# Window attention on one core: 256 key tiles computed off ScalarE in two other ways

## The chip, the cores and the metric

One core of one Trainium2 chip. The metric is the device time of one execution in microseconds (us); lower is better. The engines are named as the profile names them: PE is TensorE (matmuls), PEld its weight loads, DVE is VectorE, ACT is ScalarE, POOL is GpSimd, SP is SyncE (here it only starts DMAs). PSUM holds what PE computes, in eight banks; POOL works on SBUF alone.

## What is computed

An image of 224 x 224 positions with 96 channels. Channels 0 to 47 attend within horizontal stripes of 8 rows, channels 48 to 95 within vertical stripes of 8 columns; a stripe has 1792 tokens, and each direction has 28 stripes.

```python
qkv = jnp.einsum('bhwc,cd->bhwd', x, wqkv)
...
ah = _softmax(jnp.einsum('bqc,bkc->bqk', qh, kh) * scale, axis=-1)
oh = jnp.einsum('bqk,bkc->bqc', ah, vh).reshape(B, H, W, C2)
...
av = _softmax(jnp.einsum('bqc,bkc->bqk', qv, kv) * scale, axis=-1)
ov = jnp.einsum('bqk,bkc->bqc', av, vv).reshape(B, nw, H, sw, C2)
...
return jnp.einsum('bhwc,cd->bhwd', o, wo)
```

The exponentials dominate: 56 stripes of 1792 x 1792 scores.

## The kernel before

**Tiles.** The work runs over 28 passes P, each with two stripes side by side (14 passes for the rows, 14 for the columns). In a pass the queries come in four chunks c of 512, 512, 512 and 256, and the 14 key blocks of 128 make 14 tiles a chunk (7 in the last, which takes two key blocks a tile). A tile is 128 keys x 512 queries x 2 stripes: 1024 numbers on each of 128 partitions. There are 28 x 49 = 1372 tiles.

**Tiles of ScalarE (1121 of them).** `do_q` emits the four score matmuls (L761) into one of two pairs of PSUM banks (0 and 1, or 2 and 3), and one ACTIVATE (L939) that writes 2 to the power of the score into one of `NPT` buffers `PT`, in bf16. `do_v` (L788) later multiplies `PT` by V and adds into the accumulator bank of the chunk.

**The other tiles (251).** They have their bits put together by DVE and POOL. `KINDS[P][c]` lists them, one letter a tile. Their scores come from L774 (`do_s`), into two of the four banks 4 to 7 (`RING`), with some rows more in the product that add constants, so that the low 16 bits of the fp32 in PSUM are the fraction of the exponent.

- Kind P (155 tiles): DVE makes q, an affine of the low 16 bits, in a buffer `qb` (`p1`, L1082); POOL squares it (L1110), adds a constant (L1111), squares again (L1106); PE computes the scores a second time with another constant; DVE adds 128 times the score to the correction and rounds to the 16 bits of a bf16 (`f`, L1087).
- Kind R (96 tiles): DVE makes q (L1082) and, in a second pass, the product of q with another affine (`p2`, L1084); POOL squares once (L1106); then the second scores and `f` as with P.
- Kinds W and Q are in the code and are not used (`NGB = 0`).

**What sets the order.** `ORDER` is one string per pass that writes PE's order out by hand: `q` a tile of ScalarE, `v` a product with V, `1` and `2` the first and second scores of another tile into two single banks (DVE then works in two halves of 512), `3` and `4` the same into two neighbouring banks (one DVE instruction of 1024), `k`, `g`, `f` the projections, the output projection and the final sums (`K` a pair of them). Between two letters a planner runs in Python as the kernel is built: it keeps a due time for each engine from constants such as `D_SQ` or `D_AF`, and from them chooses the order of the work on DVE (`dve_step`) and POOL (`pool_step`). The constants never run on the chip; they set orders alone. Every engine's queue is in order, and semaphores hold an instruction until its inputs are there.

A product with V needs 128 rows of PE and a score 64, so PE alternates between two tilings: letters q, 1 to 4 and f are one, v, k and g the other. POOL also does the normalisation of finished stripes (L1045), and SP starts the loads, transposes and stores.

## Time and profile before

| | |
|---|---|
| median of 3 runs | 1047.13 us (1046.86 to 1047.49) |
| profiled execution, its own time | 1047.03 us |
| its span, first to last instruction | 1045.2 us |
| busy: PE, DVE, ACT, POOL | 1024.8, 1027.6, 1034.9, 1001.9 us |
| ACTIVATEs of tiles (L939) | 1121, 1030.3 us together |
| tiles off ScalarE | 251 (155 P, 96 R) |
| DMA | 96.84 MB, mean 93 GB/s |
| granted TensorE clock | 0.999 |

A row of instruction groups reads: line, engine, operation, output <- inputs, shapes, count | busy time of the group, mean ns of one | idle time of the engine just before them, and what ended it. Busy time counts overlapping instructions of a group once, while the mean is that of single ones: where the next instruction starts before the last is wholly written, 1121 instructions of 1091 ns take 1030 us. So the price of one more instruction is the step from start to start, not its mean duration.

### The profile page before, as it was taken

To read this page: it belongs to the slowest core of one execution; us is meant where nothing else is said; L and a number is where in the kernel's file an instruction comes from. 1 tells how busy PE (TensorE), PEld (TensorE's weight loads), DVE (VectorE), ACT (ScalarE), POOL (GpSimd) and SP (SyncE) were. 2 spreads that over 40 slices of the span, in tenths; PEclk is the share of its full clock that TensorE was granted. 3 is DMA by queue.
4 is the path that set the end of the run, shared out by engine and by line. 5 is a ranking of instruction groups with operands and counts; after the bars stand their busy time and mean duration, and the time that the engine had idled before them with its cause. 6 is when DMAs were issued, how large, how long until landed. Compare 5 with 4: busy or idle time off the path is not lost.

```text
span 1045.2 us, 33013 instructions
## 1 busy us (share of the span) xinstructions
PE 1024.8 (98%) x13456; PEld 388.6 (37%) x13456; DVE 1027.6 (98%) x1905; ACT 1034.9 (99%) x1131; POOL 1001.9 (96%) x662
## 2 busy tenths in 40 slices
PE   9999999999999999999999999999999999999997
PEld 4333333333333333333333333334333333343333
DVE  8999999999999999999999999999999999999998
ACT  8999999999999999999999999999999999999997
POOL 7999999999999999999999999999999999999997
PEclk9999999999999999999999999999999999999999
DMA  8997718828863774132146355534525542552343
GB/s 175 166 181 126 131 24 140 119 52 125 147 93 71 130 108 81 28 59 59 15 91 114 60 93 103 101 58 94 95 49 104 105 100 44 104 102 49 71 79 60
DMA packets 414199, 96.84 MB, mean 93 GB/s; under 512 B 404928, under 2 KB 411296, under 8 KB 414048
## 3 DMA queue, kind: packets, MB, share of 16 engines
q1 hardware_dynamic: 413376, 94.11, 51.9%
q8 instruction: 105, 1.72, 0.7%
q10 hardware_dynamic: 544, 0.44, 0.1%
q14 instruction: 46, 0.38, 0.1%
q0 software_dynamic: 128, 0.20, 0.1%
HBM read 28.31 MB, written 28.21 MB: 54 GB/s over the span
## 4 chain that ended last, share of the span: by engine, by line
PE 59%; DVE 24%; ACT 8%; issue 4%; POOL 4%; DMA 1%; POOLq 0%; ACTq 0%; SPq 0%; DVEq 0%
PE ps L788 23%; PE ps L761 20%; PE ps L774 10%; ACT PT L939 8%; DVE qb L1082 7%; DVE PT L1087 7%; DVE PT L1084 3%; PE ps L589 3%; DVE KT_sb L594 2%; PE ps L703 2%; POOL PT L1106 2%; PE ps L634 2%; DVE OT_sb L958 1%; DVE QT_sb L603 1%; POOL PT L1110 1%
## 5 line engine op out<-in xcount | busy, mean ns | idle before, releaser
L939 ACT ACTIVATE PT<-ps 128x1024 bf16<-128x1024 f32 x1121 | 1030.3, 1091 | 0.6 <-PE ps L761 0.2
L1106 POOL TENSOR_TENSOR PT<-PT 128x1024 f16<-128x1024 f16 x251 | 470.4, 1893 | 8.6 <-DVE PT L1084 1.0
L788 PE MATMUL ps<-PT,V_sb 128*49 128x512 bf16 (+1 forms) x3136 | 470.1, 362 | 0.3 <-DVE PT L1087 0.2
L761 PE MATMUL ps<-QT_sb,KT_sb 49*64 49x512 bf16 (+1 forms) x5292 | 456.4, 361 | 2.6 <-ACT PT L939 1.5
L1082 DVE TENSOR_SCALAR qb<-ps 128x512 f16<-128x512 int16 x490 | 329.8, 697 | 3.2 <-PE ps L761 0.3
L1087 DVE SCALAR_TENSOR_TENSOR PT<-ps,PT 128x512 uint16<-128x512 f32 (+1 forms) x479 | 323.0, 709 | 5.2 <-PE ps L774 0.9
L1110 POOL TENSOR_TENSOR PT<-qb 128x1024 f16<-128x1024 f16 x155 | 291.9, 1892 | 9.8 <-DVE qb L1082 6.5
L761 PEld LDWEIGHTS ps<-QT_sb,KT_sb 49*64 49x64 bf16 x5292 | 136.9, 104 | 264.0 <-ACT PT L939 240.3
L774 PE MATMUL ps<-QT_sb,KT_sb 54*64 54x512 bf16 (+1 forms) x2008 | 202.6, 394 | 11.7 <-DVE PT L1087 2.7
L788 PEld LDWEIGHTS ps<-PT,V_sb 128*49 128x49 bf16 x3136 | 133.2, 103 | 202.6 <-issue 169.8
L1111 POOL TENSOR_SCALAR PT<-PT 128x1024 f16<-128x1024 f16 x155 | 161.8, 1044 | 13.0
L1084 DVE SCALAR_TENSOR_TENSOR PT<-ps,qb 128x512 f16<-128x512 int16 (+1 forms) x190 | 128.0, 688 | 0.6
L774 PEld LDWEIGHTS ps<-QT_sb,KT_sb 54*64 54x64 bf16 (+1 forms) x2008 | 56.8, 103 | 101.0 <-DVE PT L1087 34.2
L958 DVE CAST OT_sb<-ps 113x512 bf16<-113x512 f32 x111 | 68.5, 617 | 0.1
L603 DVE CAST QT_sb<-ps 128x512 bf16<-128x512 f32 (+1 forms) x111 | 67.5, 615 | 0.1
L594 DVE TENSOR_SCALAR_CACHE_REDUCE KT_sb<-ps 128x512 bf16<-128x512 f32 x108 | 64.4, 616 | 0.0
L709 DVE CAST og<-ps 128x480 bf16<-128x480 f32 x84 | 50.8, 616 | 0.2
L641 DVE CAST V_sb<-ps 128x480 bf16<-128x480 f32 (+1 forms) x84 | 50.8, 617 | 0.1
L589 PE MATMUL ps<-xT_sb,wq_sb 97*64 97x512 bf16 x224 | 41.5, 368 | 0.0
L589 PE MATMUL ps<-xT_sb,w_sb 97*64 97x512 bf16 x224 | 39.8, 369 | 0.0
L634 PEld LDWEIGHTS ps<-w_sb,xT_sb 96*64 96x64 bf16 x1568 | 33.6, 112 | 16.3 <-issue 7.5
L634 PE MATMUL ps<-w_sb,xT_sb 96*64 96x48 bf16 x1568 | 39.3, 190 | 0.0
(67 smaller groups left out, 236.4 us busy)
## 6 DMA issues: line engine op xcount, KB each, us to landing
xT_sb<-xt_dram SPq DMA_DIRECT2D x28, 336.0 KB, 5.2
out_dram<-og SPq DMA_DIRECT2D x190, 48.0 KB, 2.0
xp_dram<-in_x_dram SPq DMA_DIRECT2D x26, 336.0 KB
oc_all<-xp_dram SPq DMA_DIRECT2D x26, 336.0 KB, 4.6
xt_dram<-xT_sb SPq DMA_DIRECT2D x26, 336.0 KB, 6.4
oh_all<-ohn SPq DMA_DIRECT2D x52, 84.0 KB, 2.7
stg<-oh_all SPq DMA_DIRECT2D x13, 336.0 KB, 4.6
xt_dram<-xT_sb SPq DMA_DIRECT2D x4, 168.0 KB, 5.1
```

What stands on the lines that cost most here:

```text
L589: ins = e.matmul(bk[64 * w:64 * w + 64, 0:qs], lhsT=lw, rhs=xT_sb[b][0:C + 1, w, q0:q0 + qs], start=True, stop=True)
L634: ins = e.matmul(bk[64 * h:64 * h + 64, j * C2:(j + 1) * C2], lhsT=xT_sb[b][0:C, w, t0:t0 + 64], rhs=w_sb[0:C, wblk(P, "v"), 0:C2], start= ...
L761: ins = e.matmul(bank(SETS[s] + w)[64 * kh:64 * kh + 64, i * t["qs"]:(i + 1) * t["qs"]], lhsT=KT_sb[b][64 * w:64 * w + CA, kt * 128 + 64 * ...
L774: ins = e.matmul(bank(bp[w])[64 * kh:64 * kh + 64, 0:512], lhsT=KT_sb[b][64 * w:64 * w + nr, kt * 128 + 64 * kh:kt * 128 + 64 * kh + 64], ...
L788: ins = e.matmul(bank(pb)[64 * w:64 * w + CA, 0:t["qs"]], lhsT=V2_sb[b][:, w, kt - NKT + NV2, :] if second else V_sb[b][:, w, kt, :], rhs= ...
L939: S.commit("act", 0.0, D_ACT, None, lambda e, s=s, slot=slot: e.activation(PT[slot][:], ps[:, 512 * SETS[s]:512 * SETS[s] + 1024], ACTF.Ex ...
L1082: fn, reads, writes = lambda e: e.tensor_scalar(q, l, m, a, ALU.mult, ALU.add), bk, qk
L1084: fn, reads, writes = lambda e: e.scalar_tensor_tensor(y.bitcast(FP16), l, -RA * 2.0 ** 16, q, ALU.add, ALU.mult), bk + qk, ptk
L1087: fn, reads, writes = lambda e: e.scalar_tensor_tensor(y.bitcast(U16), f, 128.0, y.bitcast(FP16), ALU.mult, ALU.add), bk + ptk, ptk
L1106: square = ("pool", D_SQ, lambda e: e.tensor_tensor(y, y, y, ALU.mult), yk + ["pser"], yk)
L1110: return [("pool", D_SQ, lambda e: e.tensor_tensor(y, q, q, ALU.mult), qk, yk), ("pool", D_AF, lambda e: e.tensor_scalar(y, y, -(QS * (RB ...
L1111: ("pool", D_AF, lambda e: e.tensor_scalar(y, y, -(QS * (RB + RA) / 2) ** 2, 1.0, ALU.add, ALU.mult), yk + ["pser"], yk),
```

## The change

- Now 256 tiles are off ScalarE: 173 of kind R, 83 of kind W, none of kind P; 1116 stay on ScalarE. `KINDS` and `ORDER` are written anew for all passes.
- Kind W: one DVE pass writes 128 times the score to an fp32 buffer `gb` (`emit_p`, branch W). POOL does the rest in five instructions (`mids_w`): an affine of the low 16 bits (every second 16-bit word of `gb`), its square, the sum of `gb` and the square in fp32, and two affines that round it to 16 bits, with constants 64 apart, into two `PT` buffers. The two words differ by half an octave. There is no second score. Each word has its own product with V; the second one's is with `V2_sb`, which is 0.707 V for the last `NV2` key blocks and which POOL makes once a pass (`emit_v2`).
- Buffers: 4 of `gb` (none before), 24 of `PT` (28), 2 of `qb` (5), 6 key blocks in `V2_sb` (1).
- POOL's TENSOR_SCALARs: (x + c) x 1 becomes (x x 1) + c, in `mids_w`, `mids` and `shifted`. In the changed kernel only W's run.
- The planner's constants of POOL change, and a step is added from a two-input instruction to a one-input one (`D_TS`).

```diff
-NGB = 0
+NGB = 4
 KINDS = [
-    ["PR", "P", "PPP", ""],
-    ["RPR", "PP", "RRPRR", ""],
...
+    ["WR", "W", "RRW", ""],
+    ["RWR", "R", "WRRRR", ""],
...
-NPT = 28
-NQB = 5
-NV2 = 1
+NPT = 24
+NQB = 2
+NV2 = 6
...
-SEMD, SEMP, SELF, SEMX = 0.15, 0.10, 0.19, 0.05
+SEMD, SEMP, SELF, SEMX = 0.15, 0.13, 0.19, 0.05
...
-D_H, D_F, D_SQ, D_AF, D_M2 = 0.604, 1.137, 1.9, 1.03, 0.055
-D_AW, D_AG = 2.1, 1.03
+D_H, D_F, D_SQ, D_AF, D_M2 = 0.604, 1.137, 1.852, 1.01, 0.055
+D_AW, D_AG, D_TS = 2.088, 1.01, 0.125
...
             c = WSHIFT * 128.0 - WK * t0 * t0
-            return [("pool", D_AF, lambda e: e.tensor_scalar(z, l, WK ** 0.5 * 2.0 ** -16, -WK ** 0.5 * t0, ALU.mult, ALU.add), gk, yk),
-                    ("pool", D_SQ, lambda e: e.tensor_tensor(z, z, z, ALU.mult), yk + ["pser"], yk),
-                    ("pool", D_AW, lambda e: e.tensor_tensor(g[:], g[:], z, ALU.add), gk + yk, gk[:2]),
-                    ("pool", D_AG, lambda e: e.tensor_scalar(y.bitcast(U16), g[:], c, 1.0, ALU.add, ALU.mult), gk, yk),
-                    ("pool", D_AG, lambda e: e.tensor_scalar(PT[tl["slot2"]][:].bitcast(U16), g[:], c + 64.0, 1.0, ALU.add, ALU.mult), gk, pt_keys(tl["slot2"]))]
+            return [("S", D_AF, lambda e: e.tensor_scalar(z, l, WK ** 0.5 * 2.0 ** -16, -WK ** 0.5 * t0, ALU.mult, ALU.add), gk, yk),
+                    ("T", D_SQ, lambda e: e.tensor_tensor(z, z, z, ALU.mult), yk + ["pser"], yk),
+                    ("T", D_AW, lambda e: e.tensor_tensor(g[:], g[:], z, ALU.add), gk + yk, gk[:2]),
+                    ("S", D_AG, lambda e: e.tensor_scalar(y.bitcast(U16), g[:], 1.0, c, ALU.mult, ALU.add), gk, yk),
+                    ("S", D_AG, lambda e: e.tensor_scalar(PT[tl["slot2"]][:].bitcast(U16), g[:], 1.0, c + 64.0, ALU.mult, ALU.add), gk, pt_keys(tl["slot2"]))]
...
+            d = m[1] + (D_TS if m[0] == "S" and tm["pk"] == "T" else 0.0)
+            tm["pk"] = m[0]
```

## The prediction

> **What bounds the kernel now.** With four engines at 96 to 99% only the steady part shows which one never waits, so I read the busy time by stretches first (after each engine's name stands its busy time in that stretch):

> ```profile
> core 0: us, PE busy (x) PEld busy (x) DVE busy (x) ACT busy (x) POOL busy (x), PEclk, DMA share, GB/s
> 9.00:50.00 41.00, 40.71 (x566) 15.64 (x564) 40.52 (x73) 40.68 (x46) 36.13 (x34) 1.00 1.07 168
> 50.00:100.00 50.00, 48.22 (x626) 17.36 (x623) 49.53 (x93) 50.00 (x56) 48.08 (x38) 1.00 0.94 165
> 100.00:300.00 200.00, 194.88 (x2422) 69.85 (x2418) 198.27 (x356) 199.87 (x218) 194.81 (x121) 1.00 0.61 98
> 300.00:520.00 220.00, 216.08 (x2730) 77.69 (x2726) 218.39 (x400) 219.99 (x241) 214.56 (x135) 1.00 0.45 74
> 520.00:540.00 20.00, 19.81 (x296) 8.40 (x296) 19.97 (x40) 20.00 (x22) 19.43 (x13) 1.00 0.70 128
> 540.00:700.00 160.00, 158.73 (x2130) 61.64 (x2126) 158.87 (x288) 160.00 (x176) 154.62 (x98) 1.00 0.44 82
> 700.00:900.00 200.00, 199.24 (x2712) 77.43 (x2710) 197.86 (x360) 200.00 (x219) 192.97 (x122) 1.00 0.47 86
> 900.00:1000.00 100.00, 99.62 (x1394) 39.56 (x1392) 98.71 (x184) 99.95 (x110) 97.31 (x61) 1.00 0.40 81
> 1000.00:1030.00 30.00, 29.91 (x370) 10.85 (x362) 29.23 (x61) 30.00 (x34) 29.05 (x20) 1.00 0.47 69
> ```

> From 50 to 1030 us ACT is idle for 0.19 us in all (its column against the lengths): it paces. DVE's visible idle from 9 to 1030 us is 9.7 us, summed in the same way. The groups of instructions give prices, and the idle ahead of each:

> ```profile
> L939 ACT ACTIVATE PT<-ps 128x1024 bf16<-128x1024 f32 x1121 | 1030.3, 1091 | 0.6 <-PE ps L761 0.2
> L761 PEld LDWEIGHTS ps<-QT_sb,KT_sb 49*64 49x64 bf16 x5292 | 136.9, 104 | 264.0 <-ACT PT L939 240.3 <-issue 7.1 <-DVE KT_sb L849 0.4
> L1106 POOL TENSOR_TENSOR PT<-PT 128x1024 f16<-128x1024 f16 x251 | 470.4, 1893 | 8.6 <-DVE PT L1084 1.0
> L1110 POOL TENSOR_TENSOR PT<-qb 128x1024 f16<-128x1024 f16 x155 | 291.9, 1892 | 9.8 <-DVE qb L1082 6.5 <-PE ps L761 0.3 <-PE ps L589 0.2
> L1111 POOL TENSOR_SCALAR PT<-PT 128x1024 f16<-128x1024 f16 x155 | 161.8, 1044 | 13.0
> L1045 POOL TENSOR_TENSOR ohn<-OT_tr,rn 128x672 bf16<-128x672 bf16 x28 | 36.7, 1314 | 0.7
> L1045 POOL TENSOR_TENSOR stg<-OT_tr,rn 128x768 bf16<-128x768 bf16 x13 | 19.2, 1473 | 0.4 <-DVE rn L1030 0.4
> L1045 POOL TENSOR_TENSOR stg<-OT_tr,rn 128x576 bf16<-128x576 bf16 x13 | 15.0, 1150 | 0.5 <-ACT PT L939 0.3
> ```

> A tile of ACT costs 1030.3 / 1121 = 0.919 us. PE is behind ACT, not ahead of it: its weight loads for scores stand 240.3 us until ACT frees a pair of banks.

> POOL's idle ahead of the rows shown is 33.0 us, and most of it is no wait. One place of the timeline (start, duration, instruction) shows the steps from start to start:

> ```profile
> 199.82 1.89 POOL L1110 TENSOR_TENSOR PT<-qb 128x1024 f16<-128x1024 f16 x1
> 201.67 1.89 POOL L1106 TENSOR_TENSOR PT<-PT 128x1024 f16<-128x1024 f16 x1
> 203.65 1.04 POOL L1111 TENSOR_SCALAR PT<-PT 128x1024 f16<-128x1024 f16 x1
> 204.77 3.74 POOL L1106 TENSOR_TENSOR PT<-PT 128x1024 f16<-128x1024 f16 x2
> 200.28 0.68 DVE L1082 TENSOR_SCALAR qb<-ps 128x512 f16<-128x512 int16 x1
> 200.88 0.41 DVE L594 TENSOR_SCALAR_CACHE_REDUCE KT_sb<-ps 128x256 bf16<-128x256 f32 x1
> ```

> A two-input instruction steps by 1.85, overlapping the next by 0.04. Ahead of a TENSOR_SCALAR the step is 1.98: entering one costs 0.13. Its own step is 1.12, 1.04 of work and a gap of 0.08. The 155 of them leave 155 x (0.09 + 0.08) = 26 us of gaps, so POOL's true slack is about 7 us of the whole run. POOL is the second bound, close behind ACT. A DVE half steps by 0.60 (200.28 to 200.88).

> **The change part by part.** Counts of tiles and letters are from KINDS and ORDER in the diff.

> ACT: 5 tiles fewer x 0.919 = **-4.6 us**. With nothing else in the way the span becomes 1045.2 - 4.6 = 1040.6. The profiled execution took 1047.03, 1.8 more than its span, and is 0.1 from the median of 1047.13; the forecast is made against it.

> PE: score products off ScalarE go from 2 x 251 = 502 to 2 x 173 + 83 = 429, W's second words add 83 products with V, ACT's tiles are 5 fewer: 5 products more. Changes to the 128-row tiling go from 1005 to 999.

> ```profile
> 1021.12 0.40 PE L788 MATMUL ps<-PT,V_sb 128*49 128x512 bf16 x2
> 1021.45 0.41 PE L774 MATMUL ps<-QT_sb,KT_sb 54*64 54x512 bf16 x4
> 1021.69 0.39 PE L761 MATMUL ps<-QT_sb,KT_sb 49*64 49x512 bf16 x4
> 1022.01 0.62 PE L788 MATMUL ps<-PT,V_sb 128*49 128x512 bf16 x4
> ```

> Within one tiling the step is 0.24, across a change 0.32 to 0.33. So 5 x 0.24 - 6 x 0.17 = +0.2 us, hidden by PE's wait for ACT.

> DVE: 239, 228 and 94 tiles went through p1, f and p2 in halves, 37 passes in one piece. Now it is 245 (171 R and 74 W), 155 and 171 in halves, 31 in one piece.

> ```profile
> L1087 DVE SCALAR_TENSOR_TENSOR PT<-ps,PT 128x512 uint16<-128x512 f32 x456 | 294.9, 683 | 4.3 <-PE ps L774 0.7 <-POOL PT L1106 0.2
> L1087 DVE SCALAR_TENSOR_TENSOR PT<-ps,PT 128x1024 uint16<-128x1024 f32 x23 | 28.1, 1223 | 0.9 <-POOL PT L1106 0.4 <-PE ps L774 0.2
> L1084 DVE SCALAR_TENSOR_TENSOR PT<-ps,qb 128x512 f16<-128x512 int16 x188 | 125.6, 683 | 0.6
> L958 DVE CAST OT_sb<-ps 113x512 bf16<-113x512 f32 x84 | 57.3, 682 | 0.0
> ```

> Halves 1122 to 1142, whole pieces 37 to 31: 20 x 0.60 - 6 x 1.14 (1.223 less the same 0.08 of overlap) = **+5.2 us**. W's pass writes fp32, which no row shows. Reads of 512 from PSUM cost 682 or 683 ns whatever the operation and the two types are, so I take 0.60; the other end, twice that for twice the bytes, would add 83 x 1.2 = 100 us, and nothing in the rows leans to it. With ACT 4.6 shorter, DVE needs 9.8 us of slack and shows 9.7. It has more than it shows: an instruction that starts up to 0.08 late still overlaps the tail of the one before, and such lateness counts as busy. So DVE is covered, though narrowly.

> POOL is where the change is decided. Two-input instructions go from 251 + 155 = 406 to 173 + 2 x 83 = 339: -67 x 1.85 = -124.0. TENSOR_SCALARs of tiles go from 155 to 3 x 83 = 249: +94 x 1.12 = +105.3. Entries into one from a two-input instruction: 120 of the 155 now (counted over the whole timeline), at most two a W and one for each V2 later (194); 45 more x 0.13 = +5.9. V2, 588 elements, is priced by L1111 less 436 elements at 0.83 ns (the slope of the MEMSETs below): 0.68 x 28 = +19.0. Sum: **+6.2 us**, before two prices that the trace does not have.

> ```profile
> L420 POOL MEMSET stg<- 128x1792 f32 x1 | 1.6, 1595 | 0.1
> L419 POOL MEMSET stg<- 128x448 f32 x1 | 0.5, 476 | 0.1
> ```

> First, the multiply-first TENSOR_SCALAR (249 + 28 = 277 of them). Upper end 1.12, the add-first row. Lower end 0.91, a MEMSET's 1595 / 1792 ns x 1024. The row's own work with the overlap of all two-input rows is 1.04 - 0.04 = 1.00. The gap after it belongs to the add-first form alone among POOL's long instructions, so I take 1.02, nearer to the rows without one: -277 x 0.10 = **-27.7** (ends -58 and 0).

> Second, the sum of fp32 and fp16 (83). Lower end 1.85, the fp16 square; upper end 2.24, two one-input passes at 1.12. I take the middle, 2.05: 83 x 0.20 = **+16.6** (ends 0 and +32).

> Together: 6.2 - 27.7 + 16.6 = **-4.9 us**, with ends at -52 and +39. As ACT ends 4.6 earlier, POOL may grow by 7.4 - 4.6 = 2.8 before it becomes the bound. So it stays just below.

> [...]

> Waits: W's both words come from POOL straight into a product with V, 166 of them, where P and R pass DVE in between. PE's queue is in order, so a late word holds every score behind it, and ACT runs dry after its two bank pairs, about 1.8 us. Now such waits are rare:

> ```profile
> PEld ps L788 <- POOL PT L1106: 2.3, 9, 0.4
> ```

> W also holds two `PT` buffers of 24 through five instructions (some 7 us of POOL); 83 in 1030 us are one every 12 us, so about two buffers on average, covered unless POOL lags. SP and the DMAs issue the same work.

> **The rivals.**

> - **Forecast: ACT keeps the pace.** Span 1040.6, time 1040.6 + 1.8 = **1042.4 us**; its own range is 1040 to 1045, for the end of the run and some bubbles. For it: ACT's 0.19 us of idle. Against: slack of DVE and POOL that ends near zero.
> - **DVE's growth is not covered**, since part of its idle time is needed to wait for PE and POOL. If all of the present idle stays, the span grows by DVE's 5.2: 1045.2 + 5.2 + 1.8 = 1052.2; halfway to the forecast the time is 1047, as before. For it: L1087 and L1084 lie ahead of the bank pairs that PE waits for, and R holds its banks for two passes. Against: the hidden tails.
> - **POOL becomes the bound by the fp32 sum** at 2.24: -4.9 + 16 = +11, 8 over the margin: 1042.4 + 8 = 1050.5. It decides from 2.14 us a sum on. For it: W's 83 sums. Against: no step in the rows depends on the type.
> - **POOL becomes the bound by the gap**, which stays at the multiply-first form (1.12): 6.2 + 16.6 - 2.8 = 20 over, 1062.4; with the dear sum as well 1078. It decides from 1.05 us an instruction on. For it: the only such row. Against: all other long rows of POOL overlap.

> **How the numbers follow.** The forecast gets 0.60, DVE 0.17, the sum 0.12, the gap 0.11. A measurement of this kernel can tell about 0.2% (2.1 us) from no change. DVE's case is split into 0.03 faster, 0.06 the same, 0.08 slower; both POOL cases are slower: faster 0.63, the same 0.06, slower 0.31. The range goes from 1039, a little below the forecast for bubbles that vanish, to 1058, over DVE's and the sum's case, and leaves out the gap and the far ends. The likeliest case alone is 1040 to 1045.

> **What would show it.** Right: L939 1116 times, again with idle time near zero between 50 and 1030 us, at 0.92 each; a TENSOR_SCALAR step near 1.00 without the gap; a sum near 2.05; DVE's W pass at 683 ns a half. Wrong: ACT idle, with PE's weight loads for products with V waiting for POOL (the two POOL cases, told apart by the two steps), or for scores waiting for DVE while POOL is idle (DVE's case).

## The result, and the profile after

The changed kernel takes **1065.11 us** (median of 6 runs, 1063.24 to 1068.49), the kernel before 1047.24 in the runs beside it: a ratio of 1.0176, 95% interval 1.0155 to 1.0196. The forecast was 1042.4, with a range of 1039 to 1058; the rival "POOL becomes the bound by the gap" had 1062.4. The profiled execution took 1063.24, its span is 1061.5.

First the busy time by stretches (PE, PEld, DVE, ACT, POOL, granted clock), after:

```profile
core 0: us, PE busy (x) PEld busy (x) DVE busy (x) ACT busy (x) POOL busy (x), PEclk, DMA share, GB/s
100.00:200.00 100.00, 96.61 (x1192) 34.83 (x1186) 96.56 (x174) 97.58 (x106) 97.14 (x66) 0.98 0.62 111
400.00:500.00 100.00, 96.72 (x1180) 34.14 (x1180) 98.39 (x182) 98.14 (x107) 97.46 (x66) 1.00 0.37 59
800.00:900.00 100.00, 98.33 (x1294) 38.01 (x1291) 97.32 (x182) 98.20 (x108) 96.85 (x66) 0.98 0.40 81
50.00:1030.00 980.00, 956.81 (x12326) 354.89 (x12326) 957.39 (x1751) 966.34 (x1046) 948.77 (x655) 0.99 0.47 87
```

From 50 to 1030 us ACT is now idle for 980 - 966.34 = 13.7 us; before it was 0.19. DVE has lost too (22.6 us idle, 9.2 before). POOL's busy column, 948.77, looks no higher than before (950.8, the sum of the prediction's rows for the same 980 us), though these 980 us now hold a smaller part of a longer run; the gaps between its instructions don't show in it, since a gap counts as idle. The chain of work that ended last, by engine, shows who sets the pace (before, then after):

```profile
PE 59%; DVE 24%; ACT 8%; issue 4%; POOL 4%; DMA 1%; POOLq 0%; ACTq 0%; SPq 0%; DVEq 0%
...
PE 41%; POOL 26%; DVE 23%; issue 5%; ACT 5%; DMA 1%; DVEq 0%; POOLq 0%; ACTq 0%
```

The groups of instructions, after (mean of one; idle time ahead and its releaser):

```profile
L939 ACT ACTIVATE PT<-ps 128x1024 bf16<-128x1024 f32 x1116 | 1032.6, 1071 | 14.7 <-PE ps L761 12.8
L1106 POOL TENSOR_TENSOR PT<-PT 128x1024 f16<-128x1024 f16 x173 | 326.4, 1895 | 4.0 <-DVE wq_sb L620 0.3
L1100 POOL TENSOR_TENSOR gb<-gb,PT 128x1024 f32<-128x1024 f32 x83 | 176.8, 2131 | 2.2
L1101 POOL TENSOR_SCALAR PT<-gb 128x1024 uint16<-128x1024 f32 x83 | 86.9, 1047 | 6.8
L1102 POOL TENSOR_SCALAR PT<-gb 128x1024 uint16<-128x1024 f32 x83 | 86.9, 1047 | 6.9
L1098 POOL TENSOR_SCALAR PT<-gb 128x1024 f16<-128x1024 uint16 x83 | 86.9, 1048 | 8.5 <-DVE gb L1067 3.1
L1067 DVE TENSOR_SCALAR gb<-ps 128x512 f32<-128x512 f32 x148 | 97.1, 683 | 1.4 <-PE ps L774 0.6
```

W's pass on DVE costs 683 ns a half, as forecast. POOL's groups show almost no idle time that another engine ended, one wait of 3.1 us for a `gb` apart: it hardly ever waits. The waits (total, times, longest) say who waits for it:

```profile
ACT PT L939 <- PE ps L761: 12.8, 24, 1.2
PEld ps L788 <- POOL PT L1102: 10.3, 20, 1.1
...
DVE PT L1087 <- POOL PT L1106: 10.0, 11, 1.4
...
PEld ps L788 <- POOL PT L1101: 3.3, 8, 0.7
```

PE's loads for the product with V wait for W's words, DVE's last pass waits for R's square, and ACT waits for the scores queued behind them. POOL's timeline (start, duration) shows at what price it works:

```profile
228.89 1.90 POOL L1106 TENSOR_TENSOR PT<-PT 128x1024 f16<-128x1024 f16 x1
230.87 1.05 POOL L1101 TENSOR_SCALAR PT<-gb 128x1024 uint16<-128x1024 f32 x1
232.00 1.05 POOL L1098 TENSOR_SCALAR PT<-gb 128x1024 f16<-128x1024 uint16 x1
233.12 1.05 POOL L1102 TENSOR_SCALAR PT<-gb 128x1024 uint16<-128x1024 f32 x1
234.25 1.89 POOL L1099 TENSOR_TENSOR PT<-PT 128x1024 f16<-128x1024 f16 x1
236.10 1.89 POOL L1106 TENSOR_TENSOR PT<-PT 128x1024 f16<-128x1024 f16 x1
237.95 2.13 POOL L1100 TENSOR_TENSOR gb<-gb,PT 128x1024 f32<-128x1024 f32 x1
...
242.42 1.89 POOL L1099 TENSOR_TENSOR PT<-PT 128x1024 f16<-128x1024 f16 x1
244.40 1.05 POOL L1102 TENSOR_SCALAR PT<-gb 128x1024 uint16<-128x1024 f32 x1
245.53 2.12 POOL L1100 TENSOR_TENSOR gb<-gb,PT 128x1024 f32<-128x1024 f32 x1
```

Into a word 1.98 (228.89 to 230.87), out of it 1.13 (233.12 to 234.25; 244.40 to 245.53): the gap of the add-first form is there in the multiply-first form too. Over the whole run the medians are 1.978 into a word, 1.127 behind it, 2.087 for the sum and 1.851 for a square; only W's first affine (L1098) steps by 1.010 to R's square (and by 1.13 to its own).

For what follows I use one number for POOL's load: for each pair of lines that follow each other on POOL, their count times the lower quartile of the step from start to start, summed from 15 us on. That is about the time that POOL needs when nothing holds it; where a pair of lines is rare, some waiting stays in it. It is **1014.5 us before and 1036.1 after**, a rise of 21.6 where the prediction had -4.9.

### The profile page after: what moved, and what is told of

Same layout as the page of the kernel before. It is cut to its first block, busy times and chain, and to the rows that moved or that the text cites. A ratio compares the mean times of both kernels' runs of the same rounds, so it can differ in the third digit from the quotient of the medians.

```text
span 1061.5 us, 32708 instructions
## 1 busy us (share of the span) xinstructions
PE 1030.2 (97%) x13310; PEld 385.1 (36%) x13310; DVE 1029.9 (97%) x1920; ACT 1037.3 (98%) x1126; POOL 1018.3 (96%) x726
## 4 chain that ended last, share of the span: by engine, by line
PE 41%; POOL 26%; DVE 23%; issue 5%; ACT 5%; DMA 1%; DVEq 0%; POOLq 0%; ACTq 0%
PE ps L788 16%; PE ps L761 14%; PE ps L774 6%; POOL PT L1106 6%; POOL gb L1100 5%; DVE PT L1087 5%; ACT PT L939 5%; POOL PT L1099 5%; DVE PT L1084 5%; DVE qb L1082 4%; POOL PT L1102 3%; POOL PT L1101 3%; POOL PT L1098 2%; DVE KT_sb L594 2%; PE ps L589 2%
## 5 line engine op out<-in xcount | busy, mean ns | idle before, releaser
L939 ACT ACTIVATE PT<-ps 128x1024 bf16<-128x1024 f32 x1116 | 1032.6, 1071 | 14.7 <-PE ps L761 12.8
L788 PE MATMUL ps<-PT,V_sb 128*49 128x512 bf16 (+1 forms) x3302 | 489.5, 364 | 5.2 <-POOL PT L1102 4.1
L761 PE MATMUL ps<-QT_sb,KT_sb 49*64 49x512 bf16 (+1 forms) x5272 | 456.6, 362 | 2.0 <-ACT PT L939 0.3
L1106 POOL TENSOR_TENSOR PT<-PT 128x1024 f16<-128x1024 f16 x173 | 326.4, 1895 | 4.0 <-DVE wq_sb L620 0.3
L1087 DVE SCALAR_TENSOR_TENSOR PT<-ps,PT 128x512 uint16<-128x512 f32 (+1 forms) x328 | 223.5, 711 | 15.1 <-POOL PT L1106 10.0
L761 PEld LDWEIGHTS ps<-QT_sb,KT_sb 49*64 49x64 bf16 x5272 | 135.9, 104 | 276.3 <-ACT PT L939 238.3
L1082 DVE TENSOR_SCALAR qb<-ps 128x512 f16<-128x512 int16 (+1 forms) x344 | 230.1, 687 | 2.0 <-PE ps L774 1.1
L1084 DVE SCALAR_TENSOR_TENSOR PT<-ps,qb 128x512 f16<-128x512 int16 (+1 forms) x344 | 227.4, 684 | 0.5
L788 PEld LDWEIGHTS ps<-PT,V_sb 128*49 128x49 bf16 x3302 | 137.7, 103 | 214.6 <-issue 172.6
L774 PE MATMUL ps<-QT_sb,KT_sb 53*64 53x512 bf16 (+2 forms) x1716 | 173.4, 394 | 16.9 <-DVE PT L1087 9.7
L1100 POOL TENSOR_TENSOR gb<-gb,PT 128x1024 f32<-128x1024 f32 x83 | 176.8, 2131 | 2.2
L1067 DVE TENSOR_SCALAR gb<-ps 128x512 f32<-128x512 f32 (+1 forms) x157 | 108.1, 714 | 1.5 <-PE ps L774 0.6
L1098 POOL TENSOR_SCALAR PT<-gb 128x1024 f16<-128x1024 uint16 x83 | 86.9, 1048 | 8.5 <-DVE gb L1067 3.1
L1102 POOL TENSOR_SCALAR PT<-gb 128x1024 uint16<-128x1024 f32 x83 | 86.9, 1047 | 6.9
L1101 POOL TENSOR_SCALAR PT<-gb 128x1024 uint16<-128x1024 f32 x83 | 86.9, 1047 | 6.8
L774 PEld LDWEIGHTS ps<-QT_sb,KT_sb 53*64 53x64 bf16 (+2 forms) x1716 | 48.6, 103 | 93.2 <-DVE PT L1087 29.5
L958 DVE CAST OT_sb<-ps 113x512 bf16<-113x512 f32 x111 | 68.3, 615 | 1.9 <-PE ps L788 1.4
L594 DVE TENSOR_SCALAR_CACHE_REDUCE KT_sb<-ps 128x512 bf16<-128x512 f32 x108 | 63.9, 617 | 0.1
```

The source lines that it names most:

```text
L761: ins = e.matmul(bank(SETS[s] + w)[64 * kh:64 * kh + 64, i * t["qs"]:(i + 1) * t["qs"]], lhsT=KT_sb[b][64 * w:64 * w + CA, kt * 128 + 64 * ...
L774: ins = e.matmul(bank(bp[w])[64 * kh:64 * kh + 64, 0:512], lhsT=KT_sb[b][64 * w:64 * w + nr, kt * 128 + 64 * kh:kt * 128 + 64 * kh + 64], ...
L788: ins = e.matmul(bank(pb)[64 * w:64 * w + CA, 0:t["qs"]], lhsT=V2_sb[b][:, w, kt - NKT + NV2, :] if second else V_sb[b][:, w, kt, :], rhs= ...
L939: S.commit("act", 0.0, D_ACT, None, lambda e, s=s, slot=slot: e.activation(PT[slot][:], ps[:, 512 * SETS[s]:512 * SETS[s] + 1024], ACTF.Ex ...
L1082: fn, reads, writes = lambda e: e.tensor_scalar(q, l, m, a, ALU.mult, ALU.add), bk, qk
L1084: fn, reads, writes = lambda e: e.scalar_tensor_tensor(y.bitcast(FP16), l, -RA * 2.0 ** 16, q, ALU.add, ALU.mult), bk + qk, ptk
```

## The experiments

**POOL as the bound: less of it, more of it, and the rivals.** Four edits of the changed kernel. `e_halfsq` squares only 512 of 1024 columns in W's second step, so half of W's corrections are left unsquared; the next two add work that nobody reads.

```diff
-e.tensor_tensor(z, z, z, ALU.mult)                                       # e_halfsq, L1099
+e.tensor_tensor(z[:, 0:512], z[:, 0:512], z[:, 0:512], ALU.mult)
+e.tensor_tensor(dum[:], ident[:, 0:64], ident[:, 0:64], ALU.mult)        # e_poolplus, on POOL, once a W tile
+e.memset(dum[:], 0.0)                                                    # e_dveplus, on DVE, 128x128 fp32, with each W copy
-e.tensor_scalar(y.bitcast(U16), g[:], 1.0, c, ALU.mult, ALU.add)         # e_bf16out, both words
+e.tensor_scalar(y, g[:], 1.0, c, ALU.mult, ALU.add)
```

> The changed kernel with W's square done over half of its columns (the other half stays unsquared), all orders the same: 83 x 0.86 = 71 us less for GpSimd, nothing else. If GpSimd is the bound: 1042 to 1046 us, with ScalarE's idle time near zero again. If DVE's growth or PE's order is the cause: within 5 us of the changed kernel's 1065.

> The changed kernel with one more GpSimd product of 128 x 64 per W tile, on nothing that others wait for: 83 x 0.25 = 20.6 us more for GpSimd. If GpSimd is the bound: 1084 to 1088 us. If it has slack left and DVE or PE is the bound: under 1070.

> The changed kernel with one more DVE memset of 128 x 128 fp32 after each of W's 157 passes: 157 x 0.13 = 20 us more for DVE. If GpSimd is the bound: 1065 to 1073. If DVE is: 1083 to 1087.

> The changed kernel with W's two words written as bf16 values in place of uint16 bits (so the words are not the exponentials); every instruction, order and wait is the same. By the steps measured on GpSimd alone only integer output makes a TENSOR_SCALAR cost 0.117 us more on entering and on leaving. Theory: GpSimd's work falls by some 24 us, to about 8 under that of the kernel before, and ScalarE paces again: 1042 to 1047 us, and the step from a second word to a square is 1.01 in place of 1.127. Rival: the gap is not from the output type in this kernel (the kernel before has it with fp16 output): within 5 us of 1065.

| run | us (median of the runs) | ratio to before, 95% |
|---|---|---|
| e_halfsq | 1043.97 | 0.9963 (0.9950 to 0.9976) |
| e_poolplus | 1094.0 | 1.0426 (1.0394 to 1.0457) |
| e_dveplus | 1063.39 | 1.0146 (1.0130 to 1.0163) |
| e_bf16out | 1065.8 | 1.0169 (1.0150 to 1.0188) |

The halved square steps by 0.997 to R's square in place of 1.851, so 83 of them take some 71 us off POOL, as expected (the load number falls by 57 alone, since POOL now waits and its rare pairs hold some of that). The loss is gone and a gain of 0.4% stands in its place, within 1.6 us of the forecast. ACT paces again; its row and its stretch in `e_halfsq`:

```profile
L939 ACT ACTIVATE PT<-ps 128x1024 bf16<-128x1024 f32 x1116 | 1027.9, 1085 | 0.7 <-PE ps L761 0.4
...
50.00:1030.00 980.00, 968.32 (x12536) 361.36 (x12534) 972.92 (x1783) 979.66 (x1065) 899.53 (x659) 1.00 0.48 89
```

More work on POOL comes through in full and more: 19 us of load cost 24 us of span in the profiled run, at a granted clock of 0.983, and 29 us in the median, above the 1084 to 1088 expected. More work on DVE, 25.9 us of it, costs nothing: DVE is not the bound of this kernel. `e_bf16out`, whose words are bf16 numbers and not the bit patterns of exponentials, was made because I took the uint16 output for the cause of the gap. The steps stayed at 1.127 and 1.980, and that theory fell.

**Was there slack on POOL before?** 155 tiny products were added to the kernel before, one to each P tile.

> The kernel before with one more GpSimd product of 128 x 2 per P tile, on nothing that others wait for: 155 x 0.14 = 22 us. By the slack of 7 us that the prediction counted for GpSimd in that kernel: 22 - 7 = 15 us more, 1062. If that slack is larger than counted (over 20): 1047 to 1050. If there is none: 1069.

1077.19 us, ratio 1.0285 (1.0228 to 1.0342); profiled span 1070.6. The load rose by 24.9 us (1014.5 to 1039.4), the span by 25.4. The time is above even the 1069 expected without slack: the 7 us that I had counted did not show at all, though part of the rise may go with the clock, 0.984 in the profiled run against 0.999.

**Moving V2 to DVE**, in the plain form and in the form that also writes an accumulator:

```diff
-S.commit("pool", 0.0, D_V2, D_V2 + SEMP, lambda e: e.tensor_scalar(..., HV, 0.0, ALU.mult, ALU.add), ...)
+S.commit("dve", 0.0, 0.3, 0.3 + SEMD, lambda e: e.tensor_scalar(..., HV, 0.0, ALU.mult, ALU.add), ...)            # e_v2dve
+S.commit("dve", 0.0, 0.7, 0.7 + SEMD, lambda e: e.tensor_scalar(..., HV, None, ..., accum_out=vacc[:, 0:1]), ...) # e_v2acc
```

> The changed kernel, nothing left out: 0.707 V is made by DVE in place of GpSimd (28 times 588 elements). GpSimd's work falls by 28 x 0.65 and the entries with it, 20.7 us by its steps. If GpSimd is the bound and DVE has slack: 1042 to 1048. [...]

> [...]

`e_v2dve` took 1070.36 us, ratio 1.0198 (1.0173 to 1.0224), `e_v2acc` 1061.06, 1.0127 (1.0112 to 1.0142). Neither came to the 1042 to 1048 expected for a DVE with slack. The first block is of `e_v2dve`, the second of `e_v2acc`: V2 on DVE, then POOL's square of R:

```profile
L1120 DVE TENSOR_SCALAR V_sb<-V_sb 128x588 bf16<-128x588 bf16 x28 | 22.0, 785 | 0.0
...
L1106 POOL TENSOR_TENSOR PT<-PT 128x1024 f16<-128x1024 f16 x173 | 326.8, 1896 | 20.6 <-DVE PT L1084 16.1 <-DVE wq_sb L620 0.2
```

```profile
L1121 DVE TENSOR_SCALAR_CACHE_REDUCE V_sb<-V_sb 128x588 bf16<-128x588 bf16 x28 | 21.0, 751 | 0.0
L1121 DVE DVE_READ_ACCUMULATOR V_sb<-V_sb 128x1 bf16 x28 | 2.3, 84 | 0.0
...
L1107 POOL TENSOR_TENSOR PT<-PT 128x1024 f16<-128x1024 f16 x173 | 326.5, 1895 | 14.9 <-DVE PT L1085 10.7 <-DVE wq_sb L621 0.5
```

Both take about 18 us of load off POOL (1018.5). POOL then waits for DVE (16.1 and 10.7 us ahead of R's square): the bound has gone over to DVE, which had 22 to 23 us added and has 42% of the chain that ended last in both, POOL 4 and 5%. A run below with nearly that load on POOL and nothing added on DVE (`e_w64p`) has a span of 1046.5; `e_v2acc` has 1060.1. So of 23.3 us on DVE 13.6 came through and about 10 were covered. The plain form is no dearer by its rows, yet 9 us slower. The single copies differ (shortest, median and longest ns; the last two rows are one copy of the plain form and POOL beside it):

```profile
L1120 DVE TENSOR_SCALAR V_sb<-V_sb x28: 301/514/1967, 15.1 to 1015.6; 128x588 bf16<-128x588 bf16 x28
...
L1121 DVE TENSOR_SCALAR_CACHE_REDUCE V_sb<-V_sb x28: 704/754/757, 15.1 to 1004.3; 128x588 bf16<-128x588 bf16 x28
...
552.33 1.97 DVE L1120 TENSOR_SCALAR V_sb<-V_sb 128x588 bf16<-128x588 bf16 x1
...
552.00 2.13 POOL L1100 TENSOR_TENSOR gb<-gb,PT 128x1024 f32<-128x1024 f32 x1
```

A plain copy takes 0.30 us at best and 1.97 at most; the longest, shown here, ends 0.17 us after the instruction of POOL beside it (554.30 against 554.13). The accumulator form takes 0.70 to 0.76 in all 28. What makes the plain copies longer is not shown, nor how much of the 9 us comes from them: the granted clock was 0.986 in the one profiled run and 0.999 in the other, and the plain form's run at 0.996 took 1065.53.

**What makes the gap.** Five kernels with POOL alone, 128x1024, each form between fp16 squares and two or three in a row; they compute nothing of the attention.

> This kernel leaves the attention out: GpSimd alone runs some 25 forms of instruction of 128 x 1024, each between fp16 squares, and zeros are written. Theory A: the gap behind a TENSOR_SCALAR belongs to a factor of exactly 1.0; forms with it step 1.127 us to the next square, whatever the order and the types, all others 1.010. Theory B: it belongs to the output type uint16 (and in the kernel before to the add-first order); then the uint16 forms step 1.127 with a factor of 128 too, and multiply-first with 1.0 in fp16 steps 1.010. Between two TENSOR_SCALARs both expect 1.126, and 0.126 on entering one. The fp32 sum with an fp16 operand should step 2.087 as in the changed kernel; if two fp32 operands cost the same, the width of the operands does not set it.

> GpSimd alone again, the attention left out. In the first such kernel every form with the constant 5243.5 had the gap and every form without it had none, and each of them but one wrote uint16; the changed kernel with bf16 output kept the gap. Theory C: the gap belongs to the added constant. Then fp16 forms with 5243.5, and if the kernel before is the same case with 14.76, step 1.125 to the next square, and uint16 forms with 0.5 step 1.01. Theory D: it belongs to output that is integer, or to input and output in one buffer: then uint16 with 0.5 steps 1.125, or the in-place forms do, and fp16 with 5243.5 steps 1.01. The last part changes one thing between two TENSOR_SCALARs with squares between them: what the state that costs 0.117 us on entering holds, constants, types, count or step, shows as a step of 1.976 in place of 1.859 into them.

> GpSimd alone, the attention left out: one fp16 form of TENSOR_SCALAR, 85 pairs of constants, with squares between. In the second such kernel the gap came and went with the constants alone: 0.5, 2 and 100 had none, 8, 16, 14.76, -1.67 and 5243.5 had it, whatever types, order or buffers. Theory E: it is a property of the value (size, or digits beyond some width); then a rule can be read off, such as all powers of two from 8 up having it, and 100 being an exception is to be explained. Theory F: it depends on what ran before, in which case equal constants at two places differ.

> GpSimd alone, the attention left out: the word-making affine of kind W written as (g + c/k) x k for eleven powers of two k, with the kernel's two constants c of 5245.2 and 5309.2, and five ways to write W's first affine. If the gap belongs to the values alone, as in the 85 pairs before (there it came with 5000 to 5312 whatever the factor, and not with 32 to 101, 8192 or 16384), some k have steps of 1.01 and 1.86 for both constants: k of 64 (82 and 83), 32 (164 and 166) or one half (10490 and 10618) are the candidates. If it belongs to uint16 output with large values after all, none has.

> GpSimd alone, the attention left out: fp32 to uint16 with the constants 5245.2 and 5309.2 given in other ways. If the gap comes from the constant as it stands in the instruction, a constant read from an SBUF column has none (step 1.01 to the square, 1.86 into it), and neither has a plain copy to uint16 nor a constant of 32, 64, 512, 8192 or 16384 (which had none with fp16 output). If the gap belongs to uint16 output, all of these have it. Of 28 sums of two constants some may be free of it.

The timeline of `m2_forms`, same types, same order of operations, x times 1.0 plus a constant: 2.0 in L31, 8.0 in L32.

```profile
26.80 1.05 POOL L31 TENSOR_SCALAR oh<-h 128x1024 f16<-128x1024 f16 x1
27.81 1.90 POOL L28 TENSOR_TENSOR oh<-h 128x1024 f16<-128x1024 f16 x1
29.67 1.05 POOL L31 TENSOR_SCALAR oh<-h 128x1024 f16<-128x1024 f16 x1
30.68 1.90 POOL L28 TENSOR_TENSOR oh<-h 128x1024 f16<-128x1024 f16 x1
...
40.54 1.89 POOL L28 TENSOR_TENSOR oh<-h 128x1024 f16<-128x1024 f16 x1
42.52 1.05 POOL L32 TENSOR_SCALAR oh<-h 128x1024 f16<-128x1024 f16 x1
43.64 1.90 POOL L28 TENSOR_TENSOR oh<-h 128x1024 f16<-128x1024 f16 x1
```

With 2.0 the step into it is 1.86 and out of it 1.01; with 8.0 it is 1.98 and 1.12. **The values of the immediate constants decide** (the step out is 1.12 to 1.13 where the gap is there, 1.01 where it is missing), and neither the order (add-first with 0.5 has no gap, multiply-first with -14.76 has it), nor the type (5243.5 has it to fp16, fp32, bf16 and uint16; 0.5 to uint16 does not), nor working in place. Of the constants tried with a factor of 1.0, it is missing for 1/128 and less, the powers of two from 1/8 to 2 with 3 and 1.1, those from 32 to 512 with 48, 50, 65 and 99 to 101, those from 8192 to 65536, and for -0.5, -1, -1.5, -2 and -100; it is there for 1/64 to 1/16, 0.1, 0.3, 4 to 31, 127, 1024 to 5312, -1.67, -4, -8 and -14.76. I found no rule that holds for all, and the factor counts as well: -1.6735 has the gap with a factor of 1.0 and none with 3.0 or with the 5.06e-5 of W's first affine, and -2.0, which has none with 1.0, has it with 2 to the -14. So a good constant can't be picked from its neighbours: none of the 46 ways of `m4_pairs` to write the two words with another factor is free of the gap, not even the candidates named beforehand (32, 64 and one half), and the 28 sums of two constants in `m5_pointer` take 3.63 us each. A constant read from a column in SBUF instead costs 1.87 in and 1.083 out. The sum's surcharge comes with the second operand more than with the type: two different fp16 operands take 2.071, fp32 and fp16 2.076, one operand squared 1.850; only two fp32 are dearer, at 2.295.

**The gap in the kernel itself.** Five edits of the two words. `e_shift` moves W's exponents by 3 octaves and not 41, so that the constants are 381.2 and 445.2; `e_const` puts 512.0 for both, so its words are not the exponentials; the other three keep the values.

```diff
-WSHIFT = 41
+WSHIFT = 3                                                                         # e_shift
-e.tensor_scalar(y.bitcast(U16), g[:], 1.0, c, ALU.mult, ALU.add)
+e.tensor_scalar(y.bitcast(U16), g[:], 1.0, 512.0, ALU.mult, ALU.add)               # e_const, both words
+e.tensor_scalar(y.bitcast(U16), g[:], kc[:, 0:1], 1.0, ALU.add, ALU.mult)          # e_ptr both words, e_w64p the first
-e.tensor_scalar(PT[tl["slot2"]][:].bitcast(U16), g[:], 1.0, c + 64.0, ALU.mult, ALU.add)
+e.tensor_scalar(PT[tl["slot2"]][:].bitcast(U16), y.bitcast(U16), 1.0, 64.0, ALU.mult, ALU.add)  # e_w64, e_w64p
```

> The changed kernel with the shift of W's exponents 3 octaves instead of 41: the constant that the two words add becomes 381.2 and 445.2 instead of 5245.2 and 5309.2, and the rows of K that carry the shift get other numbers. Nothing else is edited. Theory (the value of the immediate constant makes the gap of 0.117 us behind a TENSOR_SCALAR, and that gap made GpSimd the bound): the step of L1101 and L1102 falls from 1.127 to about 1.01, 166 x 0.117 = 19 us, and the entries into them from 1.978 to 1.86, some 8 us more; ScalarE's idle time falls from 23.5 to a few us and the time to 1043 to 1047. Rival (the gap hangs on the data, the fp32 input or the uint16 output in this kernel): steps stay, time 1063 to 1067. Second rival (VectorE is as much the bound as GpSimd): steps fall, but the time stays above 1052.

> The changed kernel with the added constant of the two words read from a column in SBUF (add first, then times 1.0) instead of an immediate. Theory: steps as in the run of the form alone, 1.083 behind and 1.87 ahead, so GpSimd falls by 166 x 0.044 = 7 us and, for some 100 entries, 100 x 0.11 = 11 us: 18 us together, and the time goes to 1045 to 1050. If the gap is not what makes GpSimd the bound: 1063 to 1067.

> The changed kernel with both words' constant replaced by 512.0, one that showed no gap between squares (1.86 into it, 1.01 behind). The words of W are then not the exponentials; all instructions, sizes, waits and transfers stay. Theory (the gap of the immediate constant made GpSimd the bound): steps of L1101 and L1102 fall by 0.117 each and some 100 entries by 0.12, 31 us in all off GpSimd, ScalarE's idle time below 5 us, time 1043 to 1047. Rival (VectorE is equally the bound): steps fall, time above 1052. Rival (in this kernel the constant is not the cause): 1063 to 1067, as with 381.2.

> The changed kernel with W's second word made from the first (word + 64, uint16 to uint16) instead of from the fp32 sum with another constant; the same values. Theory: the instruction with +64 has no gap, so 83 x 0.117 behind it and 0.12 for each of some 45 entries fall away, 15 us of GpSimd; time about 1050 (slope 1, as with the constant in a column). If the new read of the first word delays PE's use of it: above 1055.

> Both at once: the first word with its constant in a column, the second word from the first with +64; the same values as the changed kernel. Theory: GpSimd falls by about 15 + 5 = 20 us, time 1045 to 1049; it would then stand at or a little below the kernel before. If changing between the two operand forms costs as much as was seen between them (1.20 against 1.13): 1050 or more.

| kernel | POOL's load, us | span, us | time, us | ratio to before, 95% |
|---|---|---|---|---|
| e_halfsq | 978.6 | 1043.0 | 1043.97 | 0.9963 (0.9950 to 0.9976) |
| e_const | 1011.6 | 1043.5 | 1045.6 | 0.9979 (0.9970 to 0.9988) |
| before (1121 tiles on ACT) | 1014.5 | 1045.2 | 1047.13 | |
| e_w64p | 1017.9 | 1046.5 | 1048.28 | 1.0006 (0.9997 to 1.0015) |
| e_w64 | 1023.1 | 1048.5 | 1050.3 | 1.0025 (1.0014 to 1.0035) |
| e_ptr | 1024.2 | 1051.8 | 1053.67 | 1.0083 (1.0051 to 1.0115) |
| e_shift | 1035.7 | 1063.1 | 1064.43 | 1.0157 (1.0144 to 1.0170) |
| after | 1036.1 | 1061.5 | 1065.11 | 1.0176 (1.0155 to 1.0196) |
| e_poolplus | 1055.2 | 1085.4 | 1094.0 | 1.0426 (1.0394 to 1.0457) |

`e_shift` missed: 381.2 has the gap (1.125 out, 1.978 in), so steps and time stayed. It says nothing against the gap as the cause, only that "32 to 512" is not the rule for its constants. `e_const` is the test: same instructions, sizes, waits and transfers, only the number that each word adds is changed. Its steps fall as expected, here for the same pair of lines as in the last rows of after's timeline:

```profile
238.86 1.90 POOL L1099 TENSOR_TENSOR PT<-PT 128x1024 f16<-128x1024 f16 x1
240.72 1.05 POOL L1102 TENSOR_SCALAR PT<-gb 128x1024 uint16<-128x1024 f32 x1
241.73 2.13 POOL L1100 TENSOR_TENSOR gb<-gb,PT 128x1024 f32<-128x1024 f32 x1
```

1.86 in and 1.01 out. The load falls by 24.5 us (the 31 expected took no account of the 1.126 that stays between a word and W's first affine), and the time by 19.5, to 1045.6: the loss becomes a gain of 0.2%. That its words are no exponentials is not the reason: those of `e_bf16out` are none either and it stayed at 1065.8, and `e_w64` and `e_w64p`, which keep the values, fall with the load too. ACT paces, as its stretch shows:

```profile
50.00:1030.00 980.00, 968.20 (x12526) 361.10 (x12526) 972.80 (x1782) 979.53 (x1065) 960.24 (x666) 1.00 0.47 89
```

`e_w64` came out where it was expected (about 1050) and `e_w64p` too (1045 to 1049). `e_ptr` fell short of its 18 us: 11.9 of load. Its rows show why: the instruction itself is longer with a column (1118 ns against 1045), and where W's first affine, with immediates, follows a word the step went up from 1.126 to 1.20.

```profile
L1105 POOL TENSOR_SCALAR PT<-gb,kc 128x1024 uint16<-128x1024 f32 x83 | 92.7, 1118 | 5.1
L1106 POOL TENSOR_SCALAR PT<-gb,kc 128x1024 uint16<-128x1024 f32 x83 | 92.7, 1118 | 1.9
```

Of the versions that keep the reference's values the best, `e_w64p`, is level with the kernel before; none beats it.

## Why the prediction was wrong

The direction was wrong, by one price on POOL. Point by point:

- **ACT**: 5 tiles fewer, and a floor near 1042.4 where nothing else binds. Right within 0.2%: `e_halfsq` at 1043.97, spans of 1043.0 and 1043.5 against 1040.6 forecast. A tile costs 1027.9 / 1116 = 0.921 there, 0.002 more than taken; over 1116 tiles that is 2 of the 2.4 us.
- **PE**: nothing in the runs speaks against +0.2, hidden; none tests it by itself.
- **DVE**: the fp32 copy at 683 ns a half was right, and so was the cover: the runs freed of POOL came to ACT's pace, and 25.9 us more on DVE did nothing in the changed kernel. About 10 us of cover, an estimate from `e_v2acc` against `e_w64p`, is near the 9.7 of visible idle time.
- **POOL, the step that failed**: "The gap after it belongs to the add-first form alone among POOL's long instructions, so I take 1.02, nearer to the rows without one: -277 x 0.10 = -27.7 (ends -58 and 0)." The upper end was the truth for the two words, 1.127. The one row with a gap, L1111, differed from the rows without one in three ways: add-first, one-input, and a constant of -14.76. I put the gap down to the first; the runs show that it was the last, and W's constants have it as well. Only W's first affine has a step of 1.01, in 41 of the 49 places where a two-input instruction follows. The 0.13 for entering a TENSOR_SCALAR hangs on the constants too: with ones that have no gap the step into it is 1.860 (`m2_forms`), 0.01 over a square's own.
- **The fp32 sum**: 2.05 taken, 2.087 measured, +3 us. Two fp32 operands take 2.295 (`m1_forms`), but W's second operand is fp16.
- **The sum of POOL** came out at +21.6 instead of -4.9. By the steps out of them, one-input instructions rose by 120.7 us (173.0 to 293.7) where the prediction had 96.6: the refused gain of 27.7, less about 4 for the 41 cheap steps. Two-input ones, sums and entries with them, fell by 99.2 where it had 101.5. Its 45 more entries do not follow from its 120 and 194, which are 74 apart; the trace of after has 175, so 55 more.
- **POOL's margin** of 2.8 us was also too large. The load table shows no corner but a bend: between 1011.6 and 1023.1 each us of load costs about 0.4 (1043.5 to 1048.5), and from there to the changed kernel one (13.0 of load, 13.0 of span), with `e_ptr` some 2 us above that. ACT's idle time from 50 to 1030 us grows with it: 0.5 us in `e_const`, 3.1 in `e_w64`, 4.9 in `e_ptr`. My reading, which no run tests by itself, is that POOL here, as it must deliver in an order written out by hand, delays others before its own total runs out.
- **The rivals**: the fourth, the gap that stays, is what happened; its 1062.4 is 2.7 below the median. That it comes so near is in part luck: it counted a margin of 2.8 us that was not there, and no cheap steps of W's first affine, about 4 us the other way. It had 0.11, too little for the only row that priced the form.

## What to carry to other kernels

Where one row alone prices an operation, list everything in which it differs from the rows it is compared with, the values of its constants too, and let the price stand until a run of that one instruction tells these apart. Sum an engine's steps from start to start rather than its busy time: POOL's busy share of the span is 96% before and after, while its load rose by 21.6 us, to 1036.1 of the 1046.5 us behind the first 15, as gaps of 0.1 us count as idle. And where another engine's order is written out by hand, the idle time of the second bound is no slack to be spent in full: here, between the runs of the table, its load cost about 0.4 us a us well before it was the bound, and one for one beyond.

## What the hardware showed beside this

```profile
L34 POOL TENSOR_SCALAR oh<-h 128x1024 f16<-128x1024 f16 x6 | 16.5, 2769 | 0.0
...
L31 POOL TENSOR_SCALAR oh<-h 128x1024 f16<-128x1024 f16 x6 | 6.2, 1045 | 0.0
```

```profile
L43 POOL TENSOR_SCALAR ou<-f 128x1024 uint16<-128x1024 f32 x4 | 14.5, 3632 | 0.3
```

- **The granted clock and the time went together**: the stretches of after above have a granted clock of 0.98 at 100 to 200 and 800 to 900 us, where before shows 1.00. The six runs of after lie between 0.997 at 1063.98 us and 0.989 at 1068.49; of the six of `e_ptr` four have 0.999 or 1.000 at 1053.5 to 1053.7, one 0.993 at 1059.39 and one 0.986 at 1065.49. That PE's waits for late words bring the clock down, and so cost more than their own length, is not shown: from 400 to 500 us PE is busy for 96.72 us, about as in the stretch from 100 on, and the clock is 1.00. The runs of after spread by 0.5%, those of before by 0.06% beside them and 0.15% in the largest set (25 runs).
